# Smaller weight pieces, earlier down products and a moved exp in a fused attention + gated-MLP kernel on one core

## The chip, the cores and the metric

The kernel runs on one core of a Trainium2 chip. The metric is the device time of one execution in microseconds (us). The profile shows one execution; its span is about 1.7 us shorter than the time of the same execution.

Engine names in the profile: PE is TensorE (matmul), PEld its weight loads, DVE is VectorE, ACT is ScalarE, POOL is GpSimd, SP is SyncE. PEclk is the clock granted to TensorE. "ps" are PSUM banks; "rg" or "ring" is the buffer that weights stream through.

## The reference, cut to what matters

```python
def reference(A_x, A_wqkv, A_wo, B_x, B_w_gate, B_w_up, B_w_down, gate_w):
    x = A_x                                            # (1, 2048, 1024)
    g = sigmoid((x * gate_w).sum(-1, keepdims=True))   # the gate
    # A: 32 heads of 32; each position looks at 8 earlier ones, 2 apart
    q, k, v = split_heads(x @ wqkv)
    a = softmax(masked(q . k_window) * scale) . v_window @ wo
    # B: gated MLP, hidden width 3584
    b = (gelu(x @ w_gate) * (x @ w_up)) @ w_down
    return g * a + (1 - g) * b
```

## The kernel before

The 2048 positions are four chunks of 512. Two chunks share one pass of gate/up (28 steps each; the first pass is chunks 0 and 1, the second chunks 2 and 3). The order on TensorE is: q, k, v of chunks 0 and 1; first gate/up; down of chunk 0; q, k, v of chunk 2; down of chunk 1; q, k, v of chunk 3; second gate/up; down of chunks 2 and 3. The gate's factors are folded into down's evacuation. Attention (the window products, softmax and sums) runs on VectorE, with its exp on ScalarE. Gate/up and down use a Strassen-like form with 7 products in place of 8, whose extra sums are VectorE work as well (the "forms": S1 to S4 for down).

The program is written as several streams of operations. A recording layer gives every operation an assumed cost, keeps a clock for each engine, and repeatedly emits the operation that could start first. **The emitted order is fixed on each engine.** So this layer decides which instructions of attention stand in front of which instructions of the matmul stream:

```python
class Weave:
    LAT = 0.1
    RATE = 320e3                       # assumed DMA bytes per us
    def _emit(self, op, t):
        if op.eng in ("SP", "POOL"):   # a transfer
            self.pipe = max(self.pipe, t) + nbytes / self.RATE
            op.end = self.pipe + 2.2
        else:
            self.clk[op.eng] = t + cost
            op.end = t + cost + op.tail
    def run(self, streams):
        # emit the head with the smallest (earliest start + bias), again and again
...
    def tt(n, f32=False):              # assumed VectorE cost of n elements
        return 0.07 + n / (960.0 if f32 else 1920.0)
...
    w.run([(0.0, main()), (0.0, loads()), (0.1, wforms()), (0.1, x_forms()),
           (0.15, preps()), (0.3, attention())])
```

The parts that the change touches. Weights stream through five slots of 8 KB per partition:

```python
    slots = [persist.tile([P, RT], BF16, name=f"rg{i}") for i in range(5)]
    ring_free = [(i, None) for i in range(5)]
```

The gate takes its exp at once, and every later step of ScalarE stands behind it:

```python
    def gate(c):
        ...                                   # 8 matmuls into a PSUM bank
        e = dve(0.63, lambda: nc.vector.transpose(out=zt[:], in_=banks[i][:]), [o])
        e = dve(0.1, lambda: nc.vector.tensor_scalar(out=zc[:], ...))
        e = act(0.1, lambda: nc.scalar.activation(out=ez[:], in_=zc[:], func=ACT.Exp),
                [e], table="exp", lag=1.0, key=("ez", c))
        yield dve(1.2, tail, [e], lag=1.0, key=("omg", c))   # 1 / (1 + ez), laid out for down
```

Each gate/up step starts with a product into one bank, a "seed" copy of it into another bank by ScalarE, and more products into both. Each step has one VectorE add that gelu needs, written here as the u2-add:

```python
    e = dve(tt(SC, True), lambda f=f: nc.vector.tensor_tensor(
            out=u2[f][:], in0=banks[Dk[f]][:], in1=u2[f][:], op=ALU.add), [o, ev[f, "u2"]])
```

Of the kernel before, what the change touches and what calls it, by code (L numbers as in the profile page):

```python
# [12 lines left out]
AP = bass.AP  # L13
# [26 lines left out]
class Weave:  # L40
# [8 lines left out]
    def __init__(self, nc, tc):  # L49
        self.nc, self.tc = nc, tc  # L50
        self.clk = {e: 0.0 for e in ("PE", "DVE", "ACT", "POOL", "SP")}
        self.pipe = 0.0
        self.table = None
        self.done = {}
        self.last = {}
        self.log = []

# [24 lines left out]
    def _emit(self, op, t):  # L82
# [15 lines left out]
        for ins in instructions[n0:] if n0 == len(instructions) else self.nc.cur_bb.bb.instructions[n0:]:  # L98
# [8 lines left out]
            self.last[eng] = ins.name  # L107
        if op.key is not None:
            self.done[op.key] = op
# [23 lines left out]
def kernel(  # L133
# [57 lines left out]
    slots = [persist.tile([P, RT], BF16, name=f"rg{i}") for i in range(5)]  # L191
# [35 lines left out]
    ring_free = [(i, None) for i in range(5)]  # L227
    held = {}

    def ring_load(key, parts, nbytes, issue):  # L230

        def pre():
            if not ring_free:
                return None
            d = ring_free[0][1]
            return () if d is None else (d,)

        def fn():
            held[key] = ring_free.pop(0)
            parts(slots[held[key][0]])  # L240
        return Op("SP", (nbytes, issue), fn, (), key=key, pre=pre)

    def ring_give(key, op):
        ring_free.append((held.pop(key)[0], op))
# [27 lines left out]
    def load_qkv(c, which, hf, pieces=1):  # L272
        def go(slot):
            wv = slot[:].rearrange("p (k n) -> p k n", k=KH)
            n = KH // pieces
            for i in range(pieces):
                nc.sync.dma_start(out=wv[:, i * n:(i + 1) * n], in_=qkv_src(which, hf * KH + i * n, n))
        return ring_load(("wqkv", c, which, hf), go, KH * P * D * 2, 0.5 * pieces)
# [23 lines left out]
    def load_block(sup, b):  # L302
        c0, c1 = b * FB * P, (b + 1) * FB * P

        def raw(slot):
            rv = slot[:].rearrange("p (u k n) -> p u k n", u=2, k=KT)
            nc.sync.dma_start(out=rv[:, 0], in_=B_w_gate[:, c0:c1].rearrange("(k p) n -> p k n", p=P))
            if sup == 0:
                nc.sync.dma_start(out=rv[:, 1], in_=B_w_up[:, c0:c1].rearrange("(k p) n -> p k n", p=P))
            else:  # L310
                nc.sync.dma_start(out=rv[:, 1, KH:KT],
                                  in_=B_w_up[D // 2:D, c0:c1].rearrange("(k p) n -> p k n", p=P))
        yield ring_load(("raw", sup, b), raw, (2 if sup == 0 else 1.5) * D * FB * P * 2, 1.0)
        if sup == 0:
            o = ring_load(("ft", sup, b), lambda slot: None, 0, 0.0)
        else:
            o = ring_load(("ft", sup, b), lambda slot: nc.sync.dma_start(out=slot[:], in_=fdram[b]),
                          4 * KH * P * FB * P * 2, 0.4)
        yield o
# [3 lines left out]
    def load_down(c, extra=()):  # L323
        extra = list(extra)
        def whole(hf, name):
            def go(slot):
                wv = slot[:, 0:7 * NW]
                k0 = hf * 7
                if name[0] == "B":
                    r0 = ((int(name[1]) - 1) * FH + k0) * P  # L330
                    nh = int(name[2]) - 1
                    nc.sync.dma_start(out=wv.rearrange("p (k n) -> p k n", k=7),
                                      in_=B_w_down[r0:r0 + 7 * P, nh * NW:(nh + 1) * NW]
                                      .rearrange("(k p) n -> p k n", p=P))
                else:
                    nc.sync.dma_start(out=wv, in_=ddram[int(name[1]) - 1][:, k0 * NW:(k0 + 7) * NW])
            return go

        for m, (_, name) in enumerate(SEQ):
            dep = [("stored", "d")] if name[0] == "T" else []  # L340
            for hf in range(2):
                o = ring_load(("wd", c, m, hf), whole(hf, name), 7 * P * NW * 2, 0.4)
                o.deps = dep
                yield o
            if m == 0:
                yield ring_load(("wo", c), lambda slot: None, 0, 0.0)

            def go(m=m, name=name):
                wot = slots[held[("wo", c)][0]][:, (m % 2) * NTH * NW:(m % 2 + 1) * NTH * NW]
                if name[0] == "B":  # L350
                    kh, nh = int(name[1]) - 1, int(name[2]) - 1
                    nc.sync.dma_start(out=wot.rearrange("p (k n) -> p k n", k=NTH),
                                      in_=AP(A_wo.tensor, A_wo.offset + kh * NTH * D + nh * NW,
                                             [[NT * D, P], [D, NTH], [1, NW]]))
                else:
                    nc.sync.dma_start(out=wot, in_=odram[int(name[1]) - 1])
            yield Op("SP", (NTH * P * NW * 2, 0.4), go,
                     ([("pr", c, m - 2, 1)] if m >= 2 else [("wo", c)]) + ([("stored", "o")] if name[0] == "T" else []),
                     key=("wom", c, m))
            if m >= 1:  # L360
                yield from extra[:2]
                extra = extra[2:]

    def loads():
        for hf in range(2):
            yield load_qkv(0, 0, hf, KH)
        yield load_prep(0)
        for hf in range(2):
            yield load_qkv(0, 1, hf)
# [14 lines left out]
        for sup in range(NSUP):  # L384
# [3 lines left out]
            if more:  # L388
                for which in range(3):
                    for hf in range(2):  # L390
                        yield load_qkv(c0 + 2, which, hf)
            yield from load_down(c0 + 1, load_x(c0 + 3, [("ffn", sup)]) if more else ())
            if more:
                for which in range(3):
                    for hf in range(2):
                        yield load_qkv(c0 + 3, which, hf)
# [27 lines left out]
    def wforms():  # L424
        for b in range(NBLK):
            def views(b=b):
                rv = slots[held[("raw", 0, b)][0]][:].rearrange("p (u k n) -> p u k n", u=2, k=KT)
                fv = slots[held[("ft", 0, b)][0]][:].rearrange("p (f k n) -> p f k n", f=4, k=KH)
                return rv, fv

            def go(f, b=b):
                rv, fv = views(b)
                o, a, c_, op = ((fv[:, 0], rv[:, 1, 0:KH], rv[:, 1, KH:KT], ALU.add),
                                (fv[:, 1], fv[:, 0], rv[:, 0, 0:KH], ALU.subtract),
                                (fv[:, 2], rv[:, 0, 0:KH], rv[:, 1, 0:KH], ALU.subtract),
                                (fv[:, 3], rv[:, 0, KH:KT], fv[:, 1], ALU.subtract))[f]
                nc.vector.tensor_tensor(out=o, in0=a, in1=c_, op=op)
            t = tt(KH * FB * P)
            for f in range(4):
                yield dve(t, lambda f=f, go=go: go(f), [("raw", 0, b), ("ft", 0, b)], key=("wf", 0, b, f), lag=0.5)  # L440
            if NSUP > 1:
                yield Op("POOL", (4 * KH * P * FB * P * 2, 0.6),
                         lambda b=b: nc.gpsimd.dma_start(out=fdram[b], in_=slots[held[("ft", 0, b)][0]][:]),
                         [("wf", 0, b, 3)], key=("wfs", 0, b))
# [21 lines left out]
    def qkv_w(c, which, kt):  # L466
        if c < 2 and which == 2:
            return vbuf[:, kt, :]
        src = 0 if c < 2 else c
        return slots[held[("wqkv", src, which, kt // KH)][0]][:, kt % KH * D:(kt % KH + 1) * D]  # L470
# [11 lines left out]
    def qkv(c, which):  # L482
        src = 0 if c < 2 else c
        dw = [("wqkv", 0, 2)] if (c < 2 and which == 2) else [("wqkv", src, which, hf) for hf in range(2)]
# [13 lines left out]
        if which < 2 and c != 0:  # L498
            for hf in range(2):
                ring_give(("wqkv", src, which, hf), o)  # L500
        elif c > 1:
            for hf in range(2):
                ring_give(("wqkv", src, which, hf), o)

    def qkv_first():
        taken = [bank_take() for t in range(NT)]
        for kt in range(KT):
            def go(kt=kt):
                for t in range(NT):
                    qkv_mm(taken[t][0], 0, 0, t, kt)  # L510
            o = pe(NT, go, [("wqkv", 0, 0, kt // KH)] + [("pt", j, kt // KH) for j in range(NST)]
                   + ([f for _, f in taken if f] if kt == 0 else []))
            yield o
        for t in range(NT):
            i = taken[t][0]
            if t % 2 == 0:
                e = act(0.48, lambda t=t, i=i: nc.scalar.copy(out=qkv_dst(0, 0, t), in_=banks[i][:]), [o],
                        key=("qkv", 0, 0, t))
            else:
                e = dve(0.6, lambda t=t, i=i: nc.vector.tensor_copy(out=qkv_dst(0, 0, t), in_=banks[i][:]), [o],  # L520
                        key=("qkv", 0, 0, t))
# [432 lines left out]
```

## Time and profile before

The median of four executions on the chip of the comparison is 768.09 us (767.33 to 768.98).

These are lines of the page of the kernel before: the span, the busy time of each engine with its share of the span and its instructions, and two rows of the span in 40 equal slices (tenths busy, and tenths of the full clock).

```profile
span 764.6 us, 9068 instructions
PE 738.1 (97%) x3345; PEld 370.3 (48%) x3413; DVE 606.3 (79%) x827; ACT 303.4 (40%) x519; POOL 48.3 (6%) x81
...
DVE  2799999999999799989999989989998933603201
PEclk9999999999999999999899999899999999999999
```

TensorE is busy for 97% of the span. VectorE's 79% hides that it is at 8 or 9 in nearly every slice up to the 32nd and then has little to do. Two slices have a lower TensorE clock.

The list of waits of TensorE, kernel before (what waited, for whom; us in total, times, longest us):

```profile
PE ps_90 L656 <- ACT ps_94 L683: 6.3, 1, 6.3
PE ps_94 L801 <- ACT ps_92 L834: 4.0, 1, 4.0
PE ps_96 L656 <- DVE hT L721: 1.8, 1, 1.8
PE ps_94 L656 <- DVE hT L721: 1.7, 1, 1.7
```

The longest one, in the timelines of TensorE, ScalarE and VectorE (start, duration, line, operation, out<-in, count, idle time before it and its releaser):

```profile
472.26 1.03 PE L656 MATMUL ps_91<-tf,rg_85 128*128 128x512 bf16 x4
479.58 1.87 PE L656 MATMUL ps_90<-xr,rg_86 128*128 128x512 bf16 x4 [6.29 <-ACT ps_94 L683]
...
478.82 0.22 ACT L545 ACTIVATE ez<-zc 128x16 f32<-128x16 f32 x1 [8.37 <-DVE zc L539]
478.95 0.58 ACT L683 COPY ps_94<-ps_90 128x512 f32<-128x512 f32 x1
...
476.73 1.23 DVE L588 TENSOR_TENSOR rb<-qo_79,kT_81 128x2048 bf16<-128x2048 bf16 x1
477.87 0.71 DVE L535 STREAM_TRANSPOSE zt<-ps_95 128x512 f32<-128x512 f32 x1
478.62 0.17 DVE L539 TENSOR_SCALAR zc<-zt 128x16 f32<-128x16 f32 x1
```

Read it from the bottom. VectorE does attention products until 477.87 us, then the gate's transpose and zc. ScalarE's ez waits 8.37 us for zc. The seed copy that TensorE needs stands behind ez in ScalarE's order. The Trainium skill, page "Perfetto Trace Analysis", section "Tensor Engine Instruction (MATMUL, LD_WEIGHTS)", calls ScalarE and VectorE strict first-in first-out; these lines agree.

The stretch goes from the last u2-add of the first gate/up to the first u2-add of the second. Here are these two adds in VectorE's timeline, kernel before, and then a window of about the same stretch: start:end, length, busy time (and instructions) of PE, PEld, DVE, ACT, POOL, then the mean clock, the DMA share and GB/s.

```profile
265.20 0.69 DVE L745 TENSOR_TENSOR u_2134<-ps_96,u_2134 128x512 f32<-128x512 f32 x1 [0.77 <-ACT u_2134 L740]
...
484.76 0.68 DVE L745 TENSOR_TENSOR u_3537<-ps_91,u_3537 128x512 f32<-128x512 f32 x1
...
265.00:485.00 220.00, 207.09 (x924) 110.63 (x940) 210.64 (x250) 56.49 (x94) 8.65 (x16) 0.97 0.75 237
```

The stretch is 484.76 - 265.20 = 219.6 us. The window holds 940 weight loads, one for each matmul (some matmul records are missing, so their count is 924). In the trace long matmuls start every 0.216 us at the full clock, and every 0.427 us at half clock; the Trainium skill, page "TensorE: Matmul & The Clock Gate", section "Wait — 56ns, not 53.3ns?", states 215.7 and 426.7 ns, which this trace agrees with. So TensorE's own work in the stretch is about 940 x 0.216 = 203 us (an estimate), and VectorE's busy time is 210 of 219.6 us. VectorE is the longer of the two here, although it is the shorter one over the span.

### The profile page before, as it was taken

The numbers are of one execution on the slowest core, as the hardware profiler recorded it, in microseconds if no ns is written. First come the engines' busy times: TensorE is split into PE (matmuls) and PEld (weight loads), VectorE is DVE, ScalarE is ACT, GpSimd is POOL, SyncE is SP. The second block draws the span as 40 slices with busy tenths as digits, with TensorE's granted clock in tenths as the row PEclk, the third lists the DMA queues.
The fourth block names the chain that finished last, engine by engine and source line by source line (L and its number), as shares of the span: only waits on it lengthen the run. The fifth ranks groups of instructions, "written<-read, shape, count | busy, mean of one in ns | idle before, by whom it ended". The sixth has DMA issues, their size and how long they took to land.

```text
span 764.6 us, 9068 instructions
## 1 busy us (share of the span) xinstructions
PE 738.1 (97%) x3345; PEld 370.3 (48%) x3413; DVE 606.3 (79%) x827; ACT 303.4 (40%) x519; POOL 48.3 (6%) x81
## 2 busy tenths in 40 slices
PE   8999989999999999999799997999999999999997
PEld 5666634444444444466344564344444444444443
DVE  2799999999999799989999989989998933603201
ACT  2333455575555811143120242575557555110110
POOL 2133310000000000100000000000000000001000
PEclk9999999999999999999899999899999999999999
DMA  9999925474553599962979844145363543889993
GB/s 310 319 331 346 338 90 192 140 218 144 187 179 124 179 325 322 332 251 77 275 233 326 293 140 149 56 138 168 122 192 104 186 145 131 289 298 328 350 309 144
DMA packets 128524, 167.84 MB, mean 220 GB/s; under 512 B 17889, under 2 KB 105953, under 8 KB 124897
## 3 DMA queue, kind: packets, MB, share of 16 engines
q1 hardware_dynamic: 122112, 139.48, 57.4%
q0 software_dynamic: 6080, 27.27, 10.0%
q8 instruction: 26, 0.43, 0.2%
q10 hardware_dynamic: 288, 0.52, 0.2%
q14 instruction: 18, 0.14, 0.1%
HBM read 135.79 MB, written 28.31 MB: 215 GB/s over the span
## 4 chain that ended last, share of the span: by engine, by line
PE 79%; DVE 10%; DMA 5%; ACT 4%; issue 2%; SPq 0%; ACTq 0%; DVEq 0%
PE ps_90 L656 5%; PE ps_91 L656 5%; PE ps_96 L656 5%; PE ps_92 L656 5%; PE ps_94 L656 5%; PE ps_89 L656 5%; PE ps_93 L656 5%; PE ps_92 L801 5%; PE ps_95 L656 4%; PE ps_89 L801 4%; PE ps_93 L801 4%; PE ps_91 L801 4%; PE ps_96 L801 4%; PE ps_94 L801 3%; PE ps_90 L801 3%; PE ps_95 L801 3%
## 5 line engine op out<-in xcount | busy, mean ns | idle before, releaser
L801 PEld LDWEIGHTS <-hT 128*128 128x128 bf16 x672 | 66.4, 99 | 85.3 <-issue 7.5
L589 DVE TENSOR_TENSOR ra<-ra,rb 128x2048 bf16<-128x2048 bf16 x56 | 68.5, 1223 | 1.3
L656 PEld LDWEIGHTS <-rg_84 128*128 128x128 bf16 x448 | 43.8, 98 | 52.9
L656 PEld LDWEIGHTS <-rg_86 128*128 128x128 bf16 x344 | 33.8, 98 | 47.3 <-issue 7.1
L656 PEld LDWEIGHTS <-rg_85 128*128 128x128 bf16 x344 | 34.0, 99 | 43.8 <-issue 4.2
L694 DVE TENSOR_TENSOR hT<-hT,gl 128x1024 bf16<-128x1024 bf16 x56 | 38.3, 684 | 18.1 <-ACT hT L691 17.9
L815 POOL DMA_DIRECT2D out_dram<-ost x24 | 13.0, 541 | 442.3 <-ACT ost L823 349.7
L639 DVE TENSOR_TENSOR rc<-ra 128x2048 bf16<-128x2048 bf16 x32 | 39.1, 1222 | 0.8
L637 DVE TENSOR_TENSOR ra<-rb,vT_83 128x2048 bf16<-128x2048 bf16 x32 | 38.1, 1218 | 0.1
L637 DVE TENSOR_TENSOR ra<-rb,vT_82 128x2048 bf16<-128x2048 bf16 x32 | 38.1, 1219 | 0.1
L588 DVE TENSOR_TENSOR rb<-qo_78,kT_80 128x2048 bf16<-128x2048 bf16 x28 | 34.2, 1222 | 2.0 <-ACT kT_80 L494 0.5
L656 PEld LDWEIGHTS <-rg_88 128*128 128x128 bf16 x216 | 21.1, 98 | 29.3 <-issue 4.2
L588 DVE TENSOR_TENSOR rb<-qo_79,kT_81 128x2048 bf16<-128x2048 bf16 x28 | 34.2, 1220 | 0.7
L656 PEld LDWEIGHTS <-rg_87 128*128 128x128 bf16 x216 | 21.1, 98 | 27.4 <-issue 2.2
L474 PEld LDWEIGHTS <-rg_86 128*128 128x128 bf16 x160 | 23.0, 144 | 11.6
L772 DVE TENSOR_TENSOR hT<-hT 128x1792 bf16<-128x1792 bf16 x16 | 17.4, 1086 | 8.7 <-PE ps_94 L801 3.8
L416 POOL DMA_DIRECT2D dforms<-hT x28 | 20.3, 725 | 49.9 <-DVE hT L407 47.4
L474 PEld LDWEIGHTS <-rg_84 128*128 128x128 bf16 x128 | 18.5, 144 | 9.9 <-issue 0.7
L474 PEld LDWEIGHTS <-rg_87 128*128 128x128 bf16 x128 | 18.2, 143 | 9.9 <-DMA rg_87<-in_A_wqkv_dram 0.8
L474 PEld LDWEIGHTS <-rg_85 128*128 128x128 bf16 x128 | 18.4, 143 | 9.3
L474 PEld LDWEIGHTS <-hT 128*128 128x128 bf16 x128 | 18.4, 143 | 9.3
L640 DVE TENSOR_TENSOR rc<-rc 128x1024 bf16<-128x1024 bf16 x32 | 22.0, 689 | 0.8
(709 smaller groups left out, 1565.1 us busy)
## 6 DMA issues: line engine op xcount, KB each, us to landing
rg_87<-dforms SPq DMA_DIRECT2D x10, 896.0 KB, 6.8
hT<-in_B_w_down_dram SPq DMA_DIRECT2D x28, 256.0 KB, 6.3
dforms<-hT POOLq DMA_DIRECT2D x28, 256.0 KB, 6.7
fforms<-rg_84 POOLq DMA_DIRECT2D x7, 1024.0 KB, 6.0
fforms<-rg_86 POOLq DMA_DIRECT2D x7, 1024.0 KB, 5.8
rg_85<-dforms SPq DMA_DIRECT2D x8, 896.0 KB, 6.3
rg_85<-fforms SPq DMA_DIRECT2D x7, 1024.0 KB, 4.8
rg_84<-fforms SPq DMA_DIRECT2D x7, 1024.0 KB, 4.8
```

Of the source, the lines that this page charges most:

```text
L416: lambda f=f: nc.gpsimd.dma_start(out=dd[:, f, r0:r0 + n, :], in_=fo[:, f]), [last],
L474: nc.tensor.matmul(banks[bk][:], lhsT=lhsT, rhs=xT(c, kt), start=(kt == 0), stop=(kt == KT - 1))
L588: yield dve(tt(n), lambda q_b=q_b, k_w=k_w: V(out=prod, in0=q_b, in1=k_w, op=ALU.mult), d, lag=0.5)
L589: yield dve(tt(n), lambda: V(out=acc, in0=acc, in1=prod, op=ALU.add))
L637: yield dve(tt(n), lambda u=u, v_w=v_w: V(out=pall[:, u], in0=ab, in1=v_w, op=ALU.mult), [("qkv", c, 2, t + u)] + halo_v, lag=0.5)
L639: yield dve(tt(n), lambda: V(out=s4, in0=pall[:, :, 0:4], in1=pall[:, :, 4:8], op=ALU.add))
L640: yield dve(tt(n // 2), lambda: V(out=s4[:, :, 0:2], in0=s4[:, :, 0:2], in1=s4[:, :, 2:4], op=ALU.add))
L656: nc.tensor.matmul(banks[bk][:], lhsT=wv[:, k, fl * P:(fl + 1) * P], rhs=rhs[:, k, :], start=(start and k == 0), stop=(k == KH - 1), skip_ ...
L694: yield dve(tt(2 * SC), lambda f=f: nc.vector.tensor_tensor(out=hT[:, :, f, :], in0=hT[:, :, f, :], in1=gl[f][:].rearrange("p (j s) -> p j ...
L772: nc.vector.tensor_tensor(out=out_[k], in0=a_[k], in1=b_[k], op=op)
L801: nc.tensor.matmul(banks[bk][:], lhsT=l, rhs=wv[:, i, :], start=(start and hf == 0 and i == 0), stop=(hf == 2 and i == NTH - 1), skip_grou ...
L815: lambda: eng.dma_start(out=o2[s0 + j * P:s0 + (j + 1) * P, nh * NW:(nh + 1) * NW], in_=ost[0][:]),
```

## The change

The intent: TensorE should stop waiting for ScalarE behind the gate's exp, should have work at the end of a gate/up pass, and should be fed by smaller loads that land sooner and free their space sooner. It has four parts:

1. **Ring.** 22 pieces of 2 KB per partition replace five slots of 8 KB. Every load, form and release works on one piece.
2. **Mid.** The first down products of the first chunk of each pass (18 matmuls for each half) stand before the last two gate/up products.
3. **Outer.** The q products of chunks 2 and 3 loop over the weight pieces outside and over the eight banks inside, so that the first needs one piece of weights instead of eight.
4. **Gate.** The gate's exp, and what follows it, move from the gate's matmuls to the chunk's attention, beside attention's first exp.

The core of the diff, with cuts:

```diff
-    slots = [persist.tile([P, RT], BF16, name=f"rg{i}") for i in range(5)]
+    NG = 22
+    GR = KH * FB * P
+    ring = persist.tile([P, NG, GR], BF16)
...
-    def load_qkv(c, which, hf, pieces=1):
...
+    def load_qkv(c, which):
+        for kt in range(KT):
+            yield ring_load(("wqkv", c, which, kt), lambda g, kt=kt: nc.sync.dma_start(
+                out=g.rearrange("p (k n) -> p k n", k=1), in_=qkv_src(which, kt, 1)))
...
     def gate(c):
-        e = act(0.1, lambda: nc.scalar.activation(out=ez[:], in_=zc[:], func=ACT.Exp), [e], table="exp", lag=1.0,
-                key=("ez", c))
-        yield e
+    def gate_exp(c):
+        ez, omg, zc = gates[c]
+        e = act(0.1, lambda: nc.scalar.activation(out=ez[:], in_=zc[:], func=ACT.Exp), [("zc", c)], table="exp", lag=1.0,
+                key=("ez", c))
+        yield e
...
     def att_half(c, a, q_, k_, v_):
         yield s
+        if a == 0:
+            yield from gate_exp(c)
         e = act(0.55, lambda: nc.scalar.activation(out=lsb, in_=lsb, func=ACT.Exp, scale=scale), [s], table="exp", lag=0.6)
         yield e
+        if a == 0:
+            yield from gate_tail(c)
...
-    def ffn(sup):
+    def ffn(sup, mid):
...
+            if i >= FT:
+                yield from mid[i - FT]
             if i >= 2:
                 f = i - 2
-                o = prod(Bk[f], "A22", T4, f, False, [ev[f, "up2"]])
+                o = yield from prod(Bk[f], "A22", T4, f, False, [ev[f, "up2"]])
...
-            yield from ffn(sup)
+            parts = down(c0)
+            yield from ffn(sup, parts)
+            yield from parts[2]
...
-                    for which in range(3):
+                    yield from qkv_outer(c + 2)
+                    for which in range(1, 3):
                         yield from qkv(c + 2, which)
                     yield from gate(c + 2)
```

A listing of the two programs' instruction orders shows the same matmuls and the same 827 VectorE instructions in both. SyncE's instructions rise from 244 to 540.

## The prediction

> **The bound now.** TensorE: 3,414 matmuls; in the timeline long ones start every 0.216 us, so 3,382 of them plus 32 short ones need about 732 us (estimate) of the 764.6 us span. About 30 us is idle or slow-clock time. By the timeline: start-up and tail 7 us; around 97 and 103 us 1.25 + 1.28; end of gate/up 1.88 (266 us) and 1.75 (649 us); 4.13 at 374 us plus 2.6 of half clock; 6.45 at 473 us plus 2.0 of half clock; 0.94 at 505 us.
>
> The three stalls at 97, 374 and 473 us have one cause. ScalarE is in order; the gate's exp (ez) waits for zc, which VectorE reaches late because it is full of attention (ScalarE waits 3.2, 9.3 and 8.4 us there), and the PSUM seed copy that TensorE needs stands behind it.
>
> **What the change does.** The instruction orders show the same matmuls and VectorE instructions.
> 1. Gate's exp moves next to attention's exp: those seed copies no longer queue behind ez. Up to 15.2 + 1.3 us.
> 2. First down products (18 matmuls, 3.9 us each) come before the last two gate/up products: hides 1.88 + 1.75.
> 3. The ring: SyncE issues rise from about 240 to 540, at 0.32-0.37 us each in the timeline: not a bound. The 7 and 8 KB rows become 2 KB. Down already streams 1 KB rows at about 300-340 GB/s without a TensorE wait. The Trainium skill ("DMA: Bandwidth & Descriptors", Specifications) puts line rate at 512 B or more; this trace does not contradict it. No loss, little gain.
> 4. Later q k-outer needs one weight piece rather than eight; no weight wait is visible there now, so about 0.
>
> **What takes some back.** VectorE is the second bound. Between the last u2-add of the first gate/up (265.2 us) and the first of the second (484.8 us), VectorE was busy 210 of 219.6 us; TensorE's work there is 940 matmuls, 203 us. Summing measured durations over the order, VectorE's chain in this stretch is 217 us before and 208 after (more attention is put off into the second gate/up), plus about 3 us of round trips to ScalarE. Of the 17 us lost here only 8-9 can return: TensorE will wait elsewhere: q's PSUM copies behind chunk 1's second exp, down 1's S2 forms, and the first steps of the second gate/up (6.9 us of VectorE work against 6.04 us of TensorE).
>
> Sum: stretch -9, around 97-103 us -2.2, end of second gate/up -1.75, other -0.5: about -13.5.
>
> **Prediction: 754 us, 745 to 763 (8 in 10). Faster by over 2%: 0.38; within 2%: 0.59; slower by over 2%: 0.03.**
>
> **What would show it.** Right: ScalarE's waits of ez on zc nearly gone from the stall list; no gap over 0.5 us at the end of either gate/up; VectorE idle under 10 us between 270 and 480 us; two or more TensorE gaps of 1-5 us whose releaser is ScalarE or VectorE in that stretch; DMA share in down as before. Wrong: TensorE gaps released by ring loads (ring pieces late), or the stretch falling to 203 us without gaps.
>
> **What would make it wrong.** Faster: VectorE's lateness hides in bank slack and the whole 20 us returns (about 747). Slower: small DMAs landing later when the early 100 us are saturated, ring order blocking loads, a long stall with half clock after it, or stores of forms (56 instead of 14 from GpSimd) holding ring pieces.

## The result, and the profile after

The median is 758.37 us (758.13 to 760.78, four executions) against 768.09 us: a ratio of 0.988, with a 95% interval of 0.9856 to 0.9904. (A ratio here is the mean time of one kernel's runs over that of the other's of the same rounds, so it is not quite the ratio of the medians quoted.) The prediction said a gain of 13.5 us with a range of 745 to 763; about 9.5 us came.

The page's lines of the kernel after that answer those of before:

```profile
span 756.4 us, 9827 instructions
PE 740.4 (98%) x3413; PEld 369.8 (49%) x3413; DVE 605.7 (80%) x827; ACT 300.6 (40%) x517; POOL 71.2 (9%) x123
...
DVE  2799999997999989989999999998998893514301
PEclk9999999999999999989999999999999999999999
```

VectorE's work is the same 606 us. TensorE's waits, kernel after:

```profile
PE ps L636 <- ACT ps L665: 5.6, 5, 4.0
PE ps L444 <- ACT qo L492: 4.9, 1, 4.9
```

The waits of before are gone, and two new ones are there. The first in time, in ScalarE's and TensorE's timelines:

```profile
332.93 0.63 ACT L591 ACTIVATE rb<-rb 128x512 f32<-128x512 f32 x1 [11.67 <-DVE rb L586]
335.95 1.99 ACT L610 COPY ra<-rc 128x1024 bf16<-128x1024 bf16 x2 [2.39 <-DVE rc L607]
337.84 3.99 ACT L492 CAST qo<-ps 128x512 bf16<-128x512 f32 x8
...
324.74 8.80 PE L444 MATMUL ps<-xr,ring 128*128 128x512 bf16 x40
338.47 11.79 PE L444 MATMUL ps<-xr,ring 128*128 128x512 bf16 x43 [4.93 <-ACT qo L492]
```

ScalarE waits 11.67 us for VectorE to reach the second exp of chunk 1's attention (line 591), and the eight copies of chunk 2's q out of PSUM stand behind it. But that exp ends at 333.56 us, just when TensorE finishes q (324.74 + 8.80 = 333.54). What holds the q copies from then on is the next step of the same attention half: two copies (line 610) that wait 2.39 us more for VectorE and take 1.99 us. So the longest wait on ScalarE is not the last blocker. The second in time, TensorE, ScalarE and VectorE:

```profile
473.78 1.03 PE L636 MATMUL ps<-xr,ring 128*128 128x512 bf16 x4
478.82 1.02 PE L636 MATMUL ps<-xr,ring 128*128 128x512 bf16 x4 [4.01 <-ACT ps L665]
...
477.65 0.63 ACT L717 ACTIVATE gl<-u 128x512 bf16<-128x512 f32 x1 [5.03 <-DVE u L713]
478.19 0.58 ACT L665 COPY ps<-ps 128x512 f32<-128x512 f32 x1
...
263.26 0.68 DVE L713 TENSOR_TENSOR u<-ps,u 128x512 f32<-128x512 f32 x1
...
476.94 0.68 DVE L713 TENSOR_TENSOR u<-ps,u 128x512 f32<-128x512 f32 x1
...
263.00:477.00 214.00, 206.88 (x947) 110.30 (x946) 201.68 (x250) 57.04 (x95) 8.63 (x16) 0.98 0.76 241
```

Line 713 is the u2-add. The stall is at the same place as the 6.3 us one before, the first steps of the second gate/up, but what it waits for is the u2-add itself: VectorE comes to it at 476.94 us. The last lines also give the stretch: 476.94 - 263.26 = 213.7 us, 5.9 us less than before.

By intervals, from the starts of the u2-adds (G0, G27, G28 and G55 are the first and last of each pass; the last column is from G55 to the end of the span):

| profile | span | start to G0 | G0 to G27 | stretch, G27 to G28 | G28 to G55 | to the end |
|---|---|---|---|---|---|---|
| before | 764.6 | 102.9 | 162.3 | 219.6 | 163.1 | 116.7 |
| after | 756.4 | 100.0 | 163.2 | 213.7 | 164.8 | 114.6 |

The stretch gave 5.9 us, the tail 2.1 us, and 2.6 us went back in the two gate/up passes. The 2.9 us before G0 are not safe: an experiment below whose order is the same there on every engine (late_v) has G0 at 102.6 us.

### The profile page after: what moved, and what is told of

Read it like the earlier page. It is cut to its first block, busy times and chain, and to the rows that moved or that the text cites. A ratio compares the mean times of both kernels' runs of the same rounds, so it can differ in the third digit from the quotient of the medians. Undisturbed runs are those within 1.5% of the kernel's fastest.

```text
span 756.4 us, 9827 instructions
## 1 busy us (share of the span) xinstructions
PE 740.4 (98%) x3413; PEld 369.8 (49%) x3413; DVE 605.7 (80%) x827; ACT 300.6 (40%) x517; POOL 71.2 (9%) x123
## 3 DMA queue, kind: packets, MB, share of 16 engines
q0 software_dynamic: 8544, 27.27, 10.2%
## 4 chain that ended last, share of the span: by engine, by line
PE 56%; DVE 20%; issue 3%; ACT 2%; DMA 2%; DVEq 0%; SPq 0%; ACTq 0%
PE ps L636 29%; PE ps L770 22%; PE ps L444 4%; DVE ra L622 3%; DVE ra L570 3%; DVE rb L569 3%; DMA ring<-in_B_w_up_dram 2%; DVE rc L624 1%; DVE u L713 1%; DVE rb L571 1%; DVE rc L625 1%; DVE hT L675 1%; DVE hT L692 1%; DMA ring<-in_A_wqkv_dram 1%; DVE hT L738 1%
## 5 line engine op out<-in xcount | busy, mean ns | idle before, releaser
L636 PEld LDWEIGHTS <-ring 128*128 128x128 bf16 x1568 | 153.8, 98 | 193.1 <-issue 9.9
L636 PE MATMUL ps<-xr,ring 128*128 128x512 bf16 x896 | 214.4, 380 | 5.6 <-ACT ps L665 5.6
L636 PE MATMUL ps<-tf,ring 128*128 128x512 bf16 x672 | 164.8, 380 | 0.0
L770 PE MATMUL ps<-ring,hT 128*128 128x512 bf16 x672 | 152.9, 379 | 0.0
L444 PE MATMUL ps<-xr,ring 128*128 128x512 bf16 x640 | 141.7, 384 | 5.0 <-ACT qo L492 4.9
L444 PEld LDWEIGHTS <-ring 128*128 128x128 bf16 x640 | 92.1, 144 | 54.2 <-issue 8.8
L622 DVE TENSOR_TENSOR ra<-rb,vT 128x2048 bf16<-128x2048 bf16 x64 | 76.1, 1218 | 0.2
L569 DVE TENSOR_TENSOR rb<-qo,kT 128x2048 bf16<-128x2048 bf16 x56 | 68.4, 1222 | 2.3 <-ACT kT L465 0.5
L770 PE MATMUL ps<-ring,qo 128*128 128x512 bf16 x192 | 49.3, 379 | 0.0
L713 DVE TENSOR_TENSOR u<-ps,u 128x512 f32<-128x512 f32 x56 | 38.4, 685 | 11.3 <-PE ps L636 8.0
L405 DVE TENSOR_TENSOR ring<-ring 128x1024 bf16<-128x1024 bf16 x56 | 37.9, 687 | 4.3 <-DMA ring<-in_B_w_up_dram 2.2
L692 DVE TENSOR_TENSOR hT<-ps,m 128x512 bf16<-128x512 f32 x56 | 38.3, 684 | 1.2 <-PE ps L636 0.9
```

The source lines that it names most:

```text
L405: nc.vector.tensor_tensor(out=g, in0=ring[:, held[("w", 0, b, x_)], :], in1=ring[:, held[("w", 0, b, y_)], :], op=op)
L444: nc.tensor.matmul(banks[bk][:], lhsT=lhsT, rhs=xT(c, kt), start=(kt == 0), stop=(kt == KT - 1))
L569: yield dve(tt(n), lambda q_b=q_b, k_w=k_w: V(out=prod, in0=q_b, in1=k_w, op=ALU.mult), d, lag=0.5)
L622: yield dve(tt(n), lambda u=u, v_w=v_w: V(out=pall[:, u], in0=ab, in1=v_w, op=ALU.mult), [("qkv", c, 2, t + u)] + halo_v, lag=0.5)
L636: nc.tensor.matmul(banks[bk][:], lhsT=wv[:, k, fl * P:(fl + 1) * P], rhs=rhs[:, k, :], start=(start and k == 0), stop=(k == KH - 1), skip_ ...
L692: ev[f, "up2"] = dve(tt(SC, True), lambda f=f: nc.vector.tensor_tensor(out=hs(f, 1), in0=v3(banks[Bk[f]][:]), in1=v3(m5[f][:]), op=ALU.add ...
```

## The experiments

Two theories were to be told apart.

- **The queue theory** (the prediction's step 1, and the change's intent): TensorE stalls because an unlucky instruction stands in ScalarE's queue, so moving that instruction returns its stall.
- **The chain theory**: in the stretch VectorE has more work placed than TensorE has, so what counts is how much of attention stands before the second gate/up's first u2-add in VectorE's order. A stall named for ScalarE only says where VectorE's lateness surfaces; it moves when the blocker is moved.

I measure the placed work as the *chain*: the sum of the trace's measured durations over all VectorE instructions that stand between G27 and G28 in the order. It is 217.7 us before and 208.4 us after. For the experiments it was from durations measured earlier and the new order; redone from each run's own trace it differs by at most 1.0 us. It is not the busy time: neighbouring durations overlap in part, and VectorE's busy time in the stretch is 210.4 us before and 201.3 us after. So the chain is an estimate of VectorE's need, and after the change, with 201.3 us busy against TensorE's 203, no run shows that VectorE by itself is the longer one; the runs show that taking work out of its chain shortens the stretch. TensorE's work in the stretch is 203 us in all; its *losses* are the sum of what the starts of its weight loads lie apart beyond 0.216 us, slow clock included. The change itself ran in the comparison above, the experiments in three later batches, each beside the kernel before; compare the ratios where a few us matter.

All kernels were correct. The kernels before of the three batches had medians of 767.54, 768.48 and 768.16 us.

| run | median us | ratio [95%] | chain | G0 | G0-27 | stretch | G28-55 | to end |
|---|---|---|---|---|---|---|---|---|
| before | 768.09 | 1 | 217.7 | 102.9 | 162.3 | 219.6 | 163.1 | 116.7 |
| after | 758.37 | 0.988 [0.9856, 0.9904] | 208.4 | 100.0 | 163.2 | 213.7 | 164.8 | 114.6 |
| gate_only | 767.60 | 0.9998 [0.997, 1.0026] | 214.0 | 101.8 | 165.1 | 216.0 | 166.2 | 117.4 |
| gate_back | 759.21 | 0.9886 [0.9868, 0.9903] | 210.1 | 103.8 | 165.5 | 210.8 | 162.4 | 114.6 |
| outer_back | 759.54 | 0.9891 [0.9872, 0.9909] | 208.4 | 101.4 | 163.0 | 213.7 | 164.4 | 114.6 |
| late_v | 754.61 | 0.9824 [0.9804, 0.9843] | 200.8 | 102.6 | 163.2 | 209.0 | 163.4 | 114.6 |
| ring_only | 756.72 | 0.985 [0.9834, 0.9867] | 204.2 | 102.9 | 165.4 | 207.7 | 162.5 | 116.4 |
| mid_back | 760.76 | 0.99 [0.9879, 0.9921] | 207.4 | 101.7 | 162.8 | 212.6 | 166.0 | 116.4 |
| exp_behind | 754.38 | 0.982 [0.9801, 0.9838] | 198.0 | 101.2 | 162.7 | 207.5 | 167.8 | 114.6 |
| exp_late_v | 746.52 | 0.971 [0.9689, 0.973] | 191.4 | 102.5 | 162.8 | 202.9 | 164.1 | 114.3 |
| before_rate | 769.50 | 1.0016 [1.0004, 1.0029] | 207.6 | 116.2 | 162.2 | 209.2 | 163.6 | 116.7 |
| before_late | 753.66 | 0.9812 [0.9797, 0.9828] | 185.1 | 102.0 | 165.1 | 204.2 | 163.8 | 116.7 |
| ring_late | 755.61 | 0.9837 [0.9822, 0.9852] | 186.3 | 102.9 | 165.3 | 204.7 | 164.1 | 116.4 |
| cost12 | 749.26 | 0.9754 [0.9739, 0.9769] | 203.8 | 99.9 | 162.1 | 207.8 | 164.4 | 114.6 |

The stretch lies between 0 and 6.0 us above the larger of the chain and 203 us in all fourteen profiles, so the chain gives the floor and not the whole length. Not every expectation of the chain theory was met: gate_only gained nothing where about 4 us were expected, gate_back's stretch came out 3 us below its range, exp_behind 1.4 us and ring_late 3.6 us slower than theirs, ring_only faster than expected; late_v and mid_back were 0.3 to 0.6 us slower than their ranges, exp_late_v 0.5 us and gate_back 0.8 us faster. before_rate's total is told below.

### gate_only: part 4 alone, on the kernel before

```diff
-        e = act(0.1, lambda: nc.scalar.activation(out=ez[:], in_=zc[:], func=ACT.Exp), [e], table="exp", ...
-        yield e
+    def gate_exp(c): ...       # as in the change
         ...
+        if a == 0:
+            yield from gate_exp(c)      # in att_half, beside attention's exp
```

> The kernel before with one part of the change: the gate's exp and its tail are issued beside attention's first exp of the same chunk. Two theories. CHAIN: between the last u2-add of the first gate/up and the first of the second, the length is set by VectorE's in-order work in that stretch (sum of measured durations over the order: 217.7 us in the kernel before, measured length 219.6; 208.4 in the changed kernel, measured 213.7; TensorE's own work there 203), so moving a blocker in ScalarE's queue only moves the wait. QUEUE: each long TensorE stall is caused by an exp that stands in ScalarE's queue ahead of a PSUM copy, and taking it away returns that stall in full. Here the order gives a chain of 214.0. CHAIN expects a stretch of 216 to 219 us, a gain of about 2 us there and 2 us at the start of the first gate/up: about 764 us. QUEUE expects the stalls of 6.7 and 8.5 us and the 1.3 us at 97 us to return: about 752 us.

The time did not move: 767.60 us, ratio 0.9998. This is the run that decides most. TensorE's longest wait, and ScalarE's timeline there:

```profile
PE ps L665 <- ACT ps L692: 17.9, 5, 11.5
...
483.58 0.63 ACT L758 ACTIVATE gl<-u 128x512 bf16<-128x512 f32 x1 [12.51 <-DVE u L754]
484.12 0.58 ACT L692 COPY ps<-ps 128x512 f32<-128x512 f32 x1
```

No ez is in the way now, and the seed copy still comes late, because a gelu stands before it that waits for the u2-add of VectorE. The stall at 374 us is gone and the one at 473 us has become 11.5 us, one seed copy later: the next place where TensorE meets VectorE. The stretch fell by 3.6 us, but the two gate/up passes got 2.8 and 3.1 us longer. Removing the named blocker returned nothing in all.

The trace of before already had a hint of this. At its 374 us stall, ScalarE's timeline has ez first and another wait for VectorE after it:

```profile
375.27 0.22 ACT L545 ACTIVATE ez<-zc 128x16 f32<-128x16 f32 x1 [9.30 <-DVE zc L539]
377.64 0.63 ACT L608 ACTIVATE rb<-rb 128x512 f32<-128x512 f32 x1 [2.15 <-DVE rb L605]
378.17 0.58 ACT L834 COPY ps_92<-ps_94 128x512 f32<-128x512 f32 x1
```

Line 834 is the seed copy that TensorE waited for. Its last blocker was attention's exp, not the gate's.

### gate_back: the change without part 4

```diff
         gates[c] = (ez, omg, zc)
+        yield from gate_exp(c)
+        yield from gate_tail(c)
...
-        if a == 0:
-            yield from gate_exp(c)
...
-        if a == 0:
-            yield from gate_tail(c)
...
-        yield dve(1.2, tail, [("ez", c)], lag=0.6, key=("omg", c))
+        yield dve(1.2, tail, [("ez", c)], lag=1.0, key=("omg", c))
```

> The changed kernel with the gate's exp and tail put back where the kernel before has them, right after the gate's matmuls. The order gives a chain of 210.1 us in the stretch (208.4 in the changed kernel). CHAIN expects a stretch of 214 to 216 us, about 1 to 2 us longer, and 2 to 3 us lost again at the start of the first gate/up: 760 to 763 us. QUEUE expects the two long stalls behind ez to come back, 12 to 15 us: 770 us or more, unless they take the place of the ones at 333 and 474 us.

759.21 us, ratio 0.9886, against the change's 758.37 us and 0.988: part 4 is worth at most about 1 us inside the change, although the prediction booked up to 16.5 us for it. The stretch is even shorter than with it (210.8 against 213.7 us), which the chain theory had not expected, and the first interval is longer (103.8 against 100.0 us). ez stands in front of the seed copy again at 474 us, but TensorE waits only 2.45 us there, not the 12 to 15 of the queue theory. (The list names a ring load for that wait; TensorE resumes 0.05 us after the seed copy behind ez ends, at 474.78 us.)

### outer_back: the change without part 3

```diff
-                    yield from qkv_outer(c + 2)
-                    for which in range(1, 3):
+                    for which in range(3):
```

> The changed kernel with q of the two later chunks computed output tile by output tile again, as in the kernel before. VectorE's chain in the stretch is the same 208.4 us; on ScalarE chunk 1's second exp now stands behind two of the eight q copies instead of in front of all eight. QUEUE (k-outer fills all eight banks and the exp then blocks all of them) expects the stall of 7.6 us at 333 us to shrink to 2 to 3 us and the total to fall by about 5 us, to 753. CHAIN expects the stall at 333 us to shrink too, but the stretch to stay at 212 to 215 us because TensorE then waits longer at the first steps of the second gate/up: 757 to 760 us.

759.54 us. The stall at 333 us is gone, since q's banks now come free one by one. The stretch is 213.7 us as in the change, and TensorE has a new stall that the change did not have:

```profile
378.58 1.03 PE L770 MATMUL ps<-ring,qo 128*128 128x512 bf16 x4
384.50 7.67 PE L770 MATMUL ps<-ring,tf 128*128 128x512 bf16 x21 [4.89 <-DVE tf L738]
```

This one is down of chunk 1 waiting for its S1 form, a VectorE instruction (line 738). The prediction had named this place, though it said the S2 forms. About the same loss surfaced 46 us later: the stall moved and the length of the stretch did not.

### late_v: move VectorE work past the stretch

Half of the v products of chunk 2's second half must wait for the first u2-add of the second gate/up. Nothing in ScalarE's queue is moved.

```diff
-                          [("qkv", c, 2, t + u)] + halo_v, lag=0.5)
+                          [("qkv", c, 2, t + u)] + halo_v
+                          + ([("g", 1, 0)] if (c, a) == (2, 1) and t >= 4 else []), lag=0.5)
```

(The key "g" is given to the u2-add.)

> The changed kernel, with the last products of chunk 2's second half of attention (the v products of tiles 4 to 7, 10 VectorE instructions) made to wait in the order for the first u2-add of the second gate/up. ScalarE's order up to the stretch's end and all work stay the same; VectorE's chain in the stretch falls from 208.4 to 200.8 us. CHAIN expects the stretch to shrink by 5 to 7 us, to 207 to 209, with the stall of 5.9 us at 474 us gone and the one of 7.6 at 333 us still there: 752 to 754 us, if the later steps of the second gate/up, which then hold the deferred work, keep up. QUEUE expects no change in the total beyond 1 to 2 us, since no exp moves: 757 to 759.

754.61 us, and the stretch 4.7 us shorter. The stall at the second gate/up is gone. The one at 333 us remains at 5.1 us, with half clock after it, and TensorE's losses in the stretch are about 7 us in all: 935 weight loads lie in it, 202 us of work, and 202 + 7 is the 209.0 us measured. So the stall in ScalarE's queue is real too, once VectorE's chain no longer hides it.

### ring_only: part 1 alone

The change with parts 2, 3 and 4 undone, by the three edits of mid_back, outer_back and gate_back together:

```diff
-            yield from ffn(sup, parts)
+            yield from ffn(sup, ((), ()))
+            yield from parts[0]
+            yield from parts[1]
...
-                    yield from qkv_outer(c + 2)
-                    for which in range(1, 3):
+                    for which in range(3):
...
         gates[c] = (ez, omg, zc)
+        yield from gate_exp(c)
+        yield from gate_tail(c)
```

> The ring of 22 pieces alone: the changed kernel with the other three parts undone (first down products after gate/up again, later q tile by tile, gate's exp after the gate's matmuls). The order puts only 204.2 us of VectorE work into the stretch (217.7 in the kernel before), because in the recording layer's own clock the stretch is 206 us with small pieces against 214 with five large ones, and attention fills whatever time that clock leaves. CHAIN expects a stretch of 209 to 212 us and about 758 us in all: the ring alone brings nearly all of the gain, although no TensorE wait on weights was seen in the stretch before. If instead the gain came from the down products and the gate's exp (3.6 and up to 16 us), the ring alone stays at 766 to 769 us.

756.72 us, ratio 0.985 [0.9834, 0.9867]. The part that the prediction booked as "no loss, little gain" gives alone about what the whole change does (758.37 us, ratio 0.988 [0.9856, 0.9904] in another batch; the intervals just overlap, so that it gives more is likely but not certain). Its stretch is 207.7 us and its chain 204.2 us, against 213.7 and 208.4 us. Against it, by the profiles, the whole change gains 2.9 us before G0 (not safe) and about 2 us in each of the first pass and the tail, and loses 6.0 us in the stretch and 2.3 us in the second pass. (ring_only keeps the rewritten code that came with the ring, down's forms in a new order among it, so it is the ring with its order and not the buffer alone.) The parts do not add: each taken out of the change alone costs at most 0.3%, and all three taken out together cost nothing.

### mid_back: the change without part 2

```diff
-            yield from ffn(sup, parts)
+            yield from ffn(sup, ((), ()))
+            yield from parts[0]
+            yield from parts[1]
```

> The changed kernel with the first down products after gate/up again. VectorE's chain in the stretch is 207.4 us. CHAIN expects the first gap at the end of gate/up to come back without costing anything in the stretch (212 to 214 us), and the second one, with VectorE idle around it, to cost its 1.8 us in full: 759 to 760.5 us. If both gaps cost their time: 762.

760.76 us; the last interval is 116.4 us instead of 114.6 us. That is the 1.75 us the prediction gave it at the end of the second pass, and it is the one part whose gain was booked right and kept. The gap at the end of the first pass came back too (2.4 us), and the stretch did not grow for it (212.6 against 213.7 us), as expected.

### exp_behind: move the other blocker

The second exp of chunk 1's attention, which stands with its two later copies in front of the copies of q at 333 us in the change, must come after them.

```diff
-        e = act(0.55, lambda: nc.scalar.activation(out=lsb, in_=lsb, func=ACT.Exp, scale=scale), [s], ...
+        e = act(0.55, lambda: nc.scalar.activation(out=lsb, in_=lsb, func=ACT.Exp, scale=scale),
+                [s] + ([("qkv", 2, 0, NT - 1)] if (c, a) == (1, 1) else []), ...
```

> The changed kernel with one dependence more in the order: chunk 1's second exp is issued after the eight q copies of chunk 2 (it lands behind two k copies as well). The order puts 198.0 us of VectorE work into the stretch. CHAIN expects 203 to 208 us there (TensorE's own work is 203, VectorE's chain about 198 + 5 of round trips + 2 of waiting for the later exp), no stall at 333 us, and 750 to 753 us in all. QUEUE expects the 7.6 us back: 751. This run does not tell the two apart; it is for a faster version.

754.38 us. The stretch fell by 6.2 us and the interval after it rose by 3.0 us; TensorE loses 10.1 us from 469 us on, first in a gap of 4.0 us at the first steps of the second gate/up and in the half clock after it. The delay of chunk 1's softmax also pushed attention back (chain 198.0 us), so this is not a pure test of the queue.

### exp_late_v: both

The constraint of exp_behind, and that of late_v for all v products of that half chunk.

```diff
+                [s] + ([("qkv", 2, 0, NT - 1)] if (c, a) == (1, 1) else [])
...
+                          + ([("g", 1, 0)] if (c, a) == (2, 1) and t >= 0 else [])
```

> The changed kernel with chunk 1's second exp behind the q copies and all the v products of chunk 2's second half after the first u2-add of the second gate/up. VectorE's chain in the stretch is 191.4 us, so TensorE should be the bound there: 203 to 206 us, and 747 to 750 us in all, if the second gate/up, which now holds 163 us of VectorE work against 163 of TensorE, keeps up; if it does not, the loss shows as TensorE gaps released by the u2-add between 480 and 560 us and the total stays at 752.

746.52 us (744.95 to 748.33), ratio 0.971 [0.9689, 0.973]: faster than both kernels. Alone the two constraints gave about 4 us each on the change; together they gave about 12, but here all v products wait and not half of them, so part of the 12 may be the wider constraint and not the pair. TensorE's waits, and the window of the stretch:

```profile
PE ps L637 <- ACT ps L666: 4.1, 5, 1.8
...
265.00:470.00 205.00, 202.88 (x926) 109.87 (x944) 186.21 (x233) 58.10 (x98) 8.64 (x16) 1.00 0.78 250
```

The stretch is 202.9 us, which is TensorE's work, and the clock is full throughout. VectorE is busy 186 of 205 us. The deferred VectorE work was done in the second gate/up pass, where it cost nothing (164.1 us against 164.8 us).

### before_rate: why does a ring move VectorE's chain?

The recording layer lets attention in wherever its clock says that VectorE is idle. If that clock thinks that the matmul stream waits for 8 KB loads, it places more attention before the second gate/up. In the layer's log, written when the program is built and not a measurement, the time from the last product h of the first gate/up pass to the first of the second is 214.0 us for the kernel before and 204.6 us for the change. The test keeps the old ring, and the order of TensorE, and changes only the assumed transfer rate:

```diff
-    RATE = 320e3
+    RATE = 3200e3
```

> The kernel before, ring and all else untouched, with one constant of the recording layer's clock changed: it believes that DMA moves ten times as much per microsecond. TensorE's and SyncE's orders come out identical; only VectorE's and ScalarE's orders differ, and VectorE's chain in the stretch falls from 217.7 to 207.6 us. If the ring's gain is the order's alone (small pieces remove waits on weights that exist only in the layer's clock), the stretch becomes 209 to 213 us and the total 757 to 761 us. If small pieces help the hardware itself, this stays at 766 to 769 us.

TensorE's and SyncE's orders are identical to the kernel before. The chain fell to 207.6 us and the stretch from 219.6 to 209.2 us, more than with the whole change. The time nevertheless stayed at 769.50 us, a miss: G0 came at 116.2 us instead of 102.9. VectorE's and TensorE's timelines show why:

```profile
32.71 0.69 DVE L407 TENSOR_TENSOR hT<-hT 128x1024 bf16<-128x1024 bf16 x1 [13.84 <-DMA hT<-in_B_w_down_dram]
...
36.71 3.60 PE L474 MATMUL ps<-xr,rg 128*128 128x512 bf16 x10 [11.14 <-DVE qo L520]
```

The layer now believed that w_down would be there early and put the forms of down's weights before the copies of q; VectorE waited 13.84 us for that load. The same mechanism that helped the stretch broke the start. Without the 13.3 us that G0 came later, the span of 768.0 us would have been 754.7 (an estimate), beside 754.8 us for ring_only; that sum is argued and no run shows it.

### before_late and ring_late: is a small piece worth anything in itself?

before_late is gate_only with both constraints of exp_late_v; ring_late is ring_only with both. VectorE does not bind in either (chains of 185 and 186 us).

```diff
 (before_late: gate_only, old ring; ring_late: ring_only, new ring; in both)
+                [s] + ([("qkv", 2, 0, NT - 1)] if (c, a) == (1, 1) else [])
+                          + ([("g", 1, 0)] if (c, a) == (2, 1) and t >= 0 else [])
```

> The kernel before, five slots of 8 KB, with the gate's exp beside attention's and the two order constraints of the fastest version so far (chunk 1's second exp after chunk 2's q copies, the v products of chunk 2's second half after the second gate/up's first u2-add). VectorE's chain in the stretch is 185.1 us, so TensorE is the bound: 203 us and 1.9 us of gap at the end of the first gate/up, 1.75 at the second. Expected 750 to 754 us. If the large slots cost something once TensorE is the bound, waits on weights appear in the list and the total is above 755.

> The ring alone (the other three parts undone) with the same two order constraints; chain 186.3 us. Expected: the fastest version's 746.5 us plus the two gaps at the ends of gate/up (1.9 and 1.75): 749 to 752 us. The difference to the fastest version is what the down products inside gate/up's end are worth when VectorE does not bind; the difference to the run with large slots is what small pieces are worth then (expected within 2 us).

753.66 and 755.61 us, stretches 204.2 and 204.7 us. The new ring is not faster than the old once VectorE is out of the way (before_late also has the gate moved). Together with before_rate's stretch this says that its gain was the order that came with it. From ring_late to exp_late_v, which adds the other three parts, the profiles' spans are 753.4 and 746.6 us and the medians, of two batches, 755.61 and 746.52: these parts are worth 7 to 9 us when the chain no longer binds (2.5 in the first pass, 1.8 in the stretch and 2.1 in the tail of the profiles), and most of that gain is invisible in the change as it was made.

### cost12: correct the layer's cost instead

VectorE's long products start 1.13 us apart when the second does not read the first, and 1.26 us apart when it does. The layer assumes 1.14 us for both. VectorE's timeline of the kernel before:

```profile
414.63 1.22 DVE L586 TENSOR_TENSOR ra<-qo_78,kT_80 128x2048 bf16<-128x2048 bf16 x1
415.76 1.22 DVE L588 TENSOR_TENSOR rb<-qo_78,kT_80 128x2048 bf16<-128x2048 bf16 x1
417.02 1.23 DVE L589 TENSOR_TENSOR ra<-ra,rb 128x2048 bf16<-128x2048 bf16 x1
```

```diff
     def tt(n, f32=False):
-        return 0.07 + n / (960.0 if f32 else 1920.0)
+        return 0.12 + n / (960.0 if f32 else 1920.0)
```

> The changed kernel with one constant of the recording layer's clock nearer to the trace: 0.12 us in place of 0.07 us of fixed cost for each VectorE instruction (a 128 x 2048 product measures 1.22 us, the layer assumed 1.14; dependent ones follow each other every 1.26 us). No explicit constraint is added. The chain in the stretch is 203.8 us. If the stalls come from the layer's optimism about VectorE, they shrink: stretch 205 to 210 us, total 749 to 755 us. If not, 757 to 760.

749.26 us, ratio 0.9754: one assumed number in the change recovers most of what exp_late_v does. Its chain is 203.8 us and its stretch 207.8 us.

## Why the prediction was right or wrong

**Right: the time, and what bounds it.** The predicted 754 us (745 to 763) holds the measured 758.37 us, and "within 2%" was the likeliest class. The statement that VectorE is the second bound in the stretch was right, and its chain was forecast as 217 and 208 us and is 217.7 and 208.4 us in the orders. late_v shows that this work matters: with only VectorE work moved, the stretch fell by 4.7 us. The stretch's term in the sum rests on these chains and not on steps 1 and 3, so the total did not come out near by luck there.

**Right: where the stalls return.** Of the three places named, the copies of q behind chunk 1's second half of attention (4.93 us at 333; its exp had just ended, two copies after it were the last blocker) and the first steps of the second gate/up (4.01 us at 474) are in the change, and down 1's forms (4.89 us at 379, S1 and not S2) in outer_back. Waits of ez are gone from ScalarE's list, no TensorE gap stands at the end of a pass, and no TensorE gap of the change is released by a ring load. DMA in the first down moved 323 GB/s (266 to 320 us) against 334 (270 to 320 us), about as before.

**Wrong: step 1, "Gate's exp moves ... Up to 15.2 + 1.3 us".** The move alone gave 0 (gate_only, ratio 0.9998), and taking it out of the change cost at most about 1 us. The prediction did cap the sum of the stretch at what VectorE allows, but it still took the gate's exp as the cause of all three stalls. At 374 us the last blocker was attention's exp. That stall is gone in gate_only, but at 473 us the u2-add stood behind the same late VectorE and the wait grew there.

**Wrong: step 3, "No loss, little gain" for the ring.** The transfers are indeed no loss. Alone, the ring gave 1.5%, about as much as the whole change. The step that failed is that a load's size was judged only by how the DMA handles it, while it also enters the layer's clock that orders VectorE. The prediction had the shorter chain in its sum, read from the order, but did not see that the ring makes it. before_rate gets the shorter stretch from the old ring by one assumed number, and before_late against ring_late shows no value of the pieces in themselves.

**Mis-sized: "stretch -9".** It was -5.9 us. The chain fell by 9.3 us as forecast, but the stretch exceeded its chain by 5.3 us after against 1.9 us before; the prediction allowed "about 3 us of round trips". VectorE idled 213.7 - 201.3 = 12.4 us there, and 11.1 us between 270 and 480 us instead of "under 10"; one single wait, at 271.5 us for a ScalarE copy, is 2.22 us. The moved exp goes with this excess: gate_back, which has it back in its old place, lies 0.7 us above its chain and 8.8 us below the stretch of before. That is one profile, and why it is so is not shown.

**Mis-sized: "other -0.5".** The two gate/up passes got longer by 0.9 and 1.7 us, a term of +2.6 us by the profiles. The second pass begins with the 4.0 us stall and half clock after it, so some of what the stretch gained was paid just after it.

**Right: "end of second gate/up -1.75".** The tail gave 2.1 us, and mid_back lost 1.8 us there again.

**Open.** Why the chain of the change (208.4 us) is longer than that of the ring alone (204.2 us) was not isolated: taking out one part leaves 207.4 to 210.1 us, and only all three together give 204.2. The term "around 97-103 us -2.2" is open too: in the profile of the change only 0.18 us of those gaps is left, but late_v and exp_late_v, in the same order up to there, have gaps of 1.4 and 1.8 us at 103 us. And 2.9 us of the profile's gain lie before G0, where programs that are the same up to there differ by as much, with waits for the first wqkv pieces that come and go between profiles (in exp_behind and late_v TensorE waits 1.6 and 1.5 us for one near 23 us; in the change none). So part of the gain before G0 may be the luck of the profiled execution.

## What to carry to other kernels

Where a schedule is recorded from assumed costs, a change of load size or of any cost is also a reordering: compare the orders on the engine with the second-most work, sum its measured durations between two synchronising points, and compare that with the first engine's work in between, before believing a share of busy time. A stall's named releaser is a place, not a price: removing it is worth only what the next blocker lets through, so a part can be worth nothing alone and something together with others (gate_only gave nothing; the three parts beside the ring cost nothing to leave out of the change, and were worth 7 to 9 us once the chain no longer bound). Put work that nothing needs yet behind the point that others wait for, and check the start of the kernel after any change to the assumed costs.

## What the Trainium skill lacked or had wrong

- "Perfetto Trace Analysis", section "Identifying Dependency Chains", tells how to find what an instruction waits for. It lacks the warning that the named wait's length is not what its removal returns: gate_only took away the named blocker of two waits of 6.3 and 4.0 us, and the ratio of the times was 0.9998, with one wait of 11.5 us in place of the two.
- "ScalarE: Activation LUTs", section "What ACT_TABLE_LOAD costs", gives 1283 ns for the load and about 1380 ns of drain, 2.66 us for each switch. The load agrees at 1.28 us. The drain does not show in ScalarE's timeline of the kernel after, where the activation starts 0.01 us after the load and the load 0.02 us after the copy before it; the switch costs about 1.3 us:

```profile
469.66 0.58 ACT L685 COPY m<-ps 128x512 f32<-128x512 f32 x1 [0.24 <-PE ps L636]
470.26 1.28 ACT L701 ACT_TABLE_LOAD   x1
471.55 0.60 ACT L701 ACTIVATE gl<-ps 128x512 bf16<-128x512 f32 x1
```

- "TensorE: Matmul & The Clock Gate", section "What's actually happening", puts the slow clock after at least one idle window of about 3.4 us. Shorter gaps of TensorE were followed by half clock here: 2.36 us (mid_back, at 266 us), 2.85 us (before_rate, at 480 us) and 3.10 us (cost12, at 461 us). One of 3.60 us (gate_back, at 328 us) was not. Half clock in mid-kernel lasted 3.4, 6.8 or 10.2 us.
- No page that I read gives the cost of two VectorE instructions in a row where the second reads the first: here 1.26 us from start to start against 1.13 us for independent ones (128x2048 bf16), and a schedule that assumed 1.14 us for both was 9 us slower (758.37 against 749.26 us, in two batches) than one that assumed 0.05 us more for each of VectorE's tensor operations.
